# Early loads, copies of V, crossbar transposes and token-tile order in a sliding-window attention plus mixer kernel

## The chip, the cores and the metric

The kernel runs on one core of a Trainium2 chip. The metric is device time in microseconds (us); lower is better. Profiles are one execution each, and their span is some 1.7 us shorter than the device time of the same execution. "PE" is TensorE, "DVE" VectorE, "ACT" ScalarE, "POOL" GpSimd and "SP" SyncE. In this kernel POOL issues the loads (they change the type from float32 to bf16) and SP issues the stores and the crossbar transposes, which are transposes done by the DMA engines. A "landing" is the time from the issue of a DMA until its data has arrived; the "granted clock" is the TensorE clock that the throttle allowed, with 1.00 as full speed.

## The reference

For 8 batches of 576 tokens, 8 heads of 64 values, attention looks back over a window of 64 tokens. Its output x (8 x 576 x 512) goes through a low-rank mixing over tokens and then a two-layer channel mixer:

```python
scores = q @ k.T / 8;  mask: 0 <= pos_q - pos_k < 64;  attn = softmax(scores)
x = attn @ v                              # heads side by side: [8, 576, 512]
u = x + (x.T @ U @ V).T                   # U: [576, 32], V: [32, 576]
out = u + relu(u @ w_ch1) @ w_ch2         # 512 -> 2048 -> 512
```

## The kernel before

The mixer works on chunks of 512 tokens, 9 in all: 16 groups of 4 matmuls (`ch1`, result `psA`), then 16 groups of 4 (`ch2`, result `psU`). Between these groups, at "slots" 0 to 32, the program puts pieces of the attention of the next batch: scores `S`, masks `M`, `PV`, the low-rank product `U`, the addition `V`, and the transposes `UT` that make `uT`, the mixer's input. Attention of batch 0 runs alone at the start; chunk 0 carries batch 1, chunk 1 carries batch 2, and so on. Batches 0 and 1 have Q and K transposed on PE; from batch 2 on it is done by crossbar transposes (`TX`, `kf`/`qf`). From batch 3 on u is transposed by the crossbar too.

```python
    w1v = moe_w_ch1.rearrange("(c p) n -> p c n", p=P)
    for lo, hi in ((0, 1024), (1024, 2048)):
        nc.gpsimd.dma_start(out=w1b[:, :, lo:hi], in_=w1v[:, :, lo:hi])
    for t in range(NFULL):                       # V of batch 0, moved between partitions
        shift_v(0, nc.gpsimd.tensor_copy, range(t, t + 1))
    for _ in load_kq(1, False):
        pass
    load_v(1)
    w2v = moe_w_ch2.rearrange("(i p) m -> p i m", p=P)
    for i in range(0, NFC, 4):
        nc.gpsimd.dma_start(out=w2b[:, i : i + 4, :], in_=w2v[:, i : i + 4, :])
    for t in range(NFULL):
        shift_v(1, nc.gpsimd.tensor_copy, range(t, t + 1))
    # ... cut ...
        return [ch1(i) for i in range(NFC)] + [ch2(t, r) for t in range(TPC) for r in range(4)]
    # ... cut ...
    PLACE = {"S": [0, 0, 0, 3, 3], "M": [0, 1, 2, 4, 5], "PV": [8], "TX": [6, 7, 8, 9, 10],
             "U": [14], "V": [16, 17, 18], "UT": [17, 17, 18, 18, 19]}
    # PLACE_1 and PLACE_2 (chunks 0 and 1) cut: PV there in five pieces
    # ... cut ...
            if b == 1:
                for _ in load_kq(2, False):
                    pass
            if b + 1 < B:
                load_v(b + 1)
            if b + 2 < B:
                for _ in load_kq(b + 2, False):
                    pass
            # ... cut ...
            if NXB <= b + 1 < B:
                place(b + 1, ("T",), {"T": where["TX"]})    # Q/K transposes, one batch ahead
```

The softmax here doesn't subtract the row's maximum and nothing guards it: scores larger than these inputs give would overflow.

Of the kernel before, what the change touches and what calls it, by code (L numbers as in the profile page):

```python
# [16 lines left out]
def kernel(  # L17
# [26 lines left out]
    NXU = 3  # L44
# [15 lines left out]
    kg_pool = ctx.enter_context(tc.tile_pool(name="kg", bufs=4))  # L60
# [30 lines left out]
    kn = [const.tile([P, NT, H, D], BF16, name=f"kn{i}") for i in range(2)]  # L91
    qn = [const.tile([P, NT, H, D], BF16, name=f"qn{i}") for i in range(2)]

    kf = const.tile([P, NT * HP * P], BF16, name="kf")
    qf = const.tile([P, NT * HP * P], BF16, name="qf")
    kt, qt = ([f[:, j * S : (j + 1) * S] for j in range(HP)] for f in (kf, qf))
    kx, qx = (f.rearrange("p (t j w) -> p t j w", t=NT, j=HP) for f in (kf, qf))
    pts = const.tile([P, HP, 2, NB - 1, W], BF16, name="pts")
    ptl = const.tile([P, HP, 2, W], BF16, name="ptl")

# [3 lines left out]
    def load_kq(b, split):  # L104
        grouped = b < NGR
        if grouped:
            kb = kg_pool.tile([GP, H, GR, D], BF16, name="kg")
            qb = kg_pool.tile([GP, H, GR, D], BF16, name="qg")
        else:
            kb, qb = kn[b % 2], qn[b % 2]  # L110
        loaded[b] = (kb, qb)
        if grouped:
            step = 4 if split else H
            for h0 in range(0, H, step):
                hs = slice(h0, h0 + step)
                for t, src in ((kb, k), (qb, q)):
                    nc.gpsimd.dma_start(  # L117
                        out=t[:, hs, :, :].rearrange("p h c d -> p h (c d)"),
                        in_=src[b, hs, :, :].rearrange("h (p c) d -> p h (c d)", c=GR),
                    )  # L120
                    yield
# [24 lines left out]
    def shift_v(b, copy, tiles):  # L146
# [4 lines left out]
        if lo < last:  # L151
            copy(out=vb[0:W, lo:last, :, :], in_=va[0:W, lo + 1 : last + 1, :, :])  # L152

# [39 lines left out]
    for i in range(2):  # L193
        nc.vector.memset(kn[i][W:P, NFULL, :, :], 0.0)
        nc.vector.memset(qn[i][W:P, NFULL, :, :], 0.0)
# [22 lines left out]
    for t in range(NFULL):  # L218
        shift_v(0, nc.gpsimd.tensor_copy, range(t, t + 1))
    for _ in load_kq(1, False):  # L220
        pass
    load_v(1)
    w2v = moe_w_ch2.rearrange("(i p) m -> p i m", p=P)
    for i in range(0, NFC, 4):
        nc.gpsimd.dma_start(out=w2b[:, i : i + 4, :], in_=w2v[:, i : i + 4, :])
    for t in range(NFULL):
        shift_v(1, nc.gpsimd.tensor_copy, range(t, t + 1))
# [10 lines left out]
    def attention(b, spare=False):  # L238
# [6 lines left out]
        pcs = {}  # L245

# [29 lines left out]
        def TQ(j):  # L276
            def f():
                copy = nc.scalar.copy if spare and j == 3 else nc.vector.tensor_copy
                copy(out=place_of(qt, j), in_=tr(qb, j, b == 1))
# [81 lines left out]
        def SC8():  # L361
            if b >= NXU:
# [226 lines left out]
        def UT(t):  # L589
            def f():  # L590
                g = g0 + t
                dst = uT_of(g // TPC)[:, g % TPC, :, :]
                if b >= NXU:
# [16 lines left out]
        pcs["S"].insert(0 if b >= NXU else HP, SC8)  # L610
        if not spare:
            pcs["M"] = [MK(j) for j in range(HP)]
            pcs["M"].insert(0 if b >= NXU else HP, MK8)
        pcs["PV"] = [PVA] if b >= NXU else [PV(t) for t in range(NT)]
# [17 lines left out]
    DVE_RELU = {0: (8, 10, 11, 13, 15), 1: (2, 4, 6, 9, 10, 12, 13)}  # L632
    DVE_RELU_N = (0, 1, 2, 4, 5, 6, 8)

    def mlp(c):
# [3 lines left out]
        def ch1(i):  # L639
            def f():  # L640
                ps = psum["mm"].tile([P, CH], FP32, name="psA", tag="mm")
                for dc in range(NDC):
                    nc.tensor.matmul(  # L643
                        ps[:],
                        w1b[:, dc, i * P : (i + 1) * P],
                        uTc[:, :, dc, :],
                        start=(dc == 0),
                        stop=(dc == NDC - 1),
                    )
                c1[i] = c1_pool.tile([P, CH], BF16, name=f"c1_{i}")  # L650
                if i in DVE_RELU.get(c, DVE_RELU_N):
                    nc.vector.tensor_relu(out=c1[i][:], in_=ps[:])  # L652
                else:
                    nc.scalar.activation(out=c1[i][:], in_=ps[:], func=ACT.Relu)  # L654
# [25 lines left out]
        return [ch1(i) for i in range(NFC)] + [ch2(t, r) for t in range(TPC) for r in range(4)]  # L680
# [6 lines left out]
        "TX": [6, 7, 8, 9, 10],  # L687
# [6 lines left out]
        "T": [11, 11, 12, 12, 13, 13, 14, 14],  # L694
        "S": [12, 13, 14, 15, 15],
        "M": [13, 14, 15, 16, 16],
        "PV": [17, 17, 18, 19, 20],
        "U": [22],
        "V": [23, 24, 25],
        "UT": [25, 26, 27, 28, 29],  # L700
        "TX": [20, 22, 24, 26, 28],
    }
    PLACE_2 = {
        "S": [8, 8, 11, 11, 13],
        "M": [9, 10, 12, 13, 14],
        "PV": [16, 16, 18, 18, 20],
        "TX": [13, 14, 15, 16, 17],
        "U": [21],
        "V": [23, 24, 25],
        "UT": [25, 26, 27, 28, 29],  # L710
    }

# [3 lines left out]
    def turn_over(n, cols=CH):  # L716
# [17 lines left out]
    pair = maskA[:, 0, 1:3, :].rearrange("p (o n) w -> p o (n w)", o=1)  # L734
    nc.vector.tensor_copy(
        out=maskA[:, 0, 3:7, :].rearrange("p (o n) w -> p o (n w)", o=2),
        in_=pair.to_broadcast([P, 2, 2 * W]),
    )
    nc.vector.tensor_copy(out=maskA[:, 0, 7, :], in_=maskA[:, 0, 1, :])
    nc.vector.tensor_scalar(  # L740
        out=maskB[:],
        in0=maskA[:, 0, :, :],
# [4 lines left out]
    )  # L747
    order = "K0 K1 B0 B1 Q0 Q1 S0 S1 K2 K3 B2 Q2 B3 Q3 S2 S3 B4 S4"
    for what in order.split():
# [7 lines left out]
        turn_over({"B1": 1, "Q1": 1, "S1": 1, "Q3": 1}.get(what, 0))  # L757
# [88 lines left out]
```

## Time and profile before

The median of the first three runs is 321.33 us (321.08 to 322.29).

| stage of the profile | from, us | length, us | PE idle in it, us |
|---|---|---|---|
| start and batch 0 | 0 | 23.7 | about 6 |
| chunk 0 (with batch 1) | 23.69 | 40.82 | 2.64 |
| chunk 1 (with batch 2) | 64.51 | 33.80 | 0.27 |
| chunk 2 (with batch 3) | 98.31 | 33.35 | 1.20 |
| chunk 3 (with batch 4) | 131.66 | 32.10 | 0.10 |

The page of the kernel before begins with the span and the busy time of each engine; part 4 is the chain of waits that ended last.

```profile
span 319.2 us, 6811 instructions
PE 304.6 (95%) x2829; PEld 148.9 (47%) x2855; DVE 163.1 (51%) x293; ACT 101.8 (32%) x160; POOL 103.2 (32%) x134
...
PE 80%; DMA 13%; POOL 5%; issue 1%; DVE 0%; POOLq 0%
```

PE is the engine to watch, so what can be won is its idle time or its work. The stretches below are chunks 0 to 3 of the kernel before. The columns are the stretch, its length, the busy time of PE, PE's weight loads, DVE, ACT and POOL (each with its number of instructions), the granted clock, the DMA share and GB/s.

```profile
23.69:64.51 40.82, 38.18 (x418) 19.27 (x423) 22.50 (x38) 16.94 (x27) 24.75 (x32) 1.00 2.02 168
64.51:98.31 33.80, 33.53 (x316) 16.31 (x318) 20.46 (x35) 12.56 (x19) 18.45 (x22) 1.00 1.91 160
98.31:131.66 33.35, 32.15 (x301) 15.09 (x301) 19.31 (x33) 10.17 (x16) 16.02 (x20) 1.00 1.88 159
131.66:163.76 32.10, 32.00 (x299) 15.22 (x302) 18.37 (x31) 10.17 (x16) 17.12 (x21) 1.00 1.83 168
```

Length less PE busy is PE's idle time: 2.64 us in chunk 0 and 1.20 us in chunk 2, nearly none in chunk 3. The table of PE's waits of the kernel before says for what:

```profile
engine line waited for: us in total, times, longest us
PE psU L665 <- DMA w2b<-in_moe_w_ch_dram: 2.3, 3, 1.1
...
PE psA L643 <- DMA uTc<-un: 1.1, 1, 1.1
...
PE psA L643 <- ACT uTc L553: 0.5, 1, 0.5
```

The first is the second weight, w2, in chunk 0. In PE's timeline the three waits stand in square brackets, each before one quarter of w2:

```profile
44.57 1.02 PE L665 MATMUL psU<-w2b,c 128*128 128x512 bf16 x4 [0.33 <-DMA w2b<-in_moe_w_ch_dram]
...
47.09 1.02 PE L665 MATMUL psU<-w2b,c 128*128 128x512 bf16 x4 [0.86 <-DMA w2b<-in_moe_w_ch_dram]
...
49.63 1.02 PE L665 MATMUL psU<-w2b,c 128*128 128x512 bf16 x3 [1.13 <-DMA w2b<-in_moe_w_ch_dram]
```

The second is at 131.66 us, between chunks 2 and 3: the mixer waits for u's crossbar transposes. The third is at 23.69 us, before the first mixer matmul.

### The profile page before, as it was taken

The page shows a single profiled execution, that of the slowest core. Times are in us where ns is not written, and L with a number is a line of the kernel's source. Part 1 is how long each engine was busy: PE and PEld are TensorE (multiplying, and loading weights), DVE is VectorE, ACT ScalarE, POOL GpSimd, SP SyncE. Part 2 cuts the span into 40 slices and gives each one's busy share as a digit, 9 for nine tenths or more (in the row PEclk, how much of TensorE's full clock was granted, in tenths as well). Part 3 has the DMA queues.
Part 4 walks back from the last instruction along what each step waited for, and adds up shares of the span by engine and source line. Part 5 has one row for each costly group of instructions (what it writes and reads, how often), then busy time and mean ns, then how long its engine had stood idle before and what let it go on. Part 6 is the DMA issues. An engine that isn't in the chain of part 4 may idle for free.

```text
span 319.2 us, 6811 instructions
## 1 busy us (share of the span) xinstructions
PE 304.6 (95%) x2829; PEld 148.9 (47%) x2855; DVE 163.1 (51%) x293; ACT 101.8 (32%) x160; POOL 103.2 (32%) x134
## 2 busy tenths in 40 slices
PE   6879988999999999899999999999999999999995
PEld 6544543544454544354445444544454444444442
DVE  4464584537675854475647454756474443016011
ACT  2645550337124440345033502350245003201500
POOL 8591696645744744555543400000000000000000
PEclk9999999999999999999999999999999999999999
DMA  7999999999999999999999994444200520020011
GB/s 103 165 225 202 153 201 171 114 185 179 148 124 218 157 127 138 193 179 156 146 204 167 138 162 150 68 100 103 98 2 2 115 100 2 11 87 33 2 66 66
DMA packets 151871, 39.56 MB, mean 124 GB/s; under 512 B 140960, under 2 KB 146080, under 8 KB 151840
## 3 DMA queue, kind: packets, MB, share of 16 engines
q0 software_dynamic: 100096, 18.36, 82.2%
q1 hardware_dynamic: 51744, 20.77, 37.0%
q8 instruction: 22, 0.36, 0.5%
q14 instruction: 9, 0.07, 0.1%
HBM read 37.14 MB, written 9.44 MB: 146 GB/s over the span
## 4 chain that ended last, share of the span: by engine, by line
PE 80%; DMA 13%; POOL 5%; issue 1%; DVE 0%; POOLq 0%
PE psU L665 36%; PE psA L643 35%; DMA qg<-in_q_dram 5%; DMA vA<-in_v_dram 3%; DMA uTc<-un 3%; PE psv L566 2%; DMA qn<-in_q_dram 2%; PE sc L326 2%; PE xw L388 2%; POOL vB L149 1%; POOL vB L152 1%; PE xr L388 1%; PE pshh L487 1%; PE tpu L598 1%; POOL kg L117 1%
## 5 line engine op out<-in xcount | busy, mean ns | idle before, releaser
L665 PE MATMUL psU<-w2b,c 128*128 128x512 bf16 x555 | 130.3, 379 | 3.6 <-DMA w2b<-in_moe_w_ch_dram 2.3
L643 PE MATMUL psA<-uTc,w1b 128*128 128x512 bf16 x576 | 131.0, 380 | 1.6 <-DMA uTc<-un 1.1
L665 PEld LDWEIGHTS <-c 128*128 128x128 bf16 x576 | 55.2, 98 | 66.8 <-issue 3.0
L643 PEld LDWEIGHTS <-w1b 128*128 128x128 bf16 x576 | 54.0, 98 | 66.3 <-DMA uTc<-un 1.6
L654 ACT ACTIVATE c<-psA 128x512 bf16<-128x512 f32 x83 | 49.6, 597 | 91.3 <-PE psA L643 91.2
L674 DVE TENSOR_TENSOR osb<-psU,un 128x512 f32<-128x512 f32 x36 | 24.9, 691 | 82.9 <-PE psU L665 82.7
L652 DVE TENSOR_SCALAR c<-psA 128x512 bf16<-128x512 f32 x61 | 42.1, 690 | 25.8 <-PE psA L643 25.8
L579 DVE TENSOR_TENSOR un<-psv,xs 128x512 bf16<-128x512 f32 (+1 forms) x40 | 25.4, 683 | 22.1 <-PE psv L566 22.0
L135 POOL DMA_DIRECT2D vA<-in_v_dram x32 | 28.1, 888 | 19.8 <-DMA kn<-in_k_dram 6.4
L126 POOL DMA_DIRECT2D qn<-in_q_dram x30 | 25.3, 843 | 22.9 <-DMA vA<-in_v_dram 12.8
L346 ACT ACTIVATE pts<-sc 128x1024 bf16<-128x1024 f32 x32 | 31.4, 1028 | 2.3 <-PE sc L326 2.2
L126 POOL DMA_DIRECT2D kn<-in_k_dram x30 | 25.8, 859 | 15.9 <-DMA vA<-in_v_dram 9.4
L379 ACT ACTIVATE ptl<-low 128x256 bf16<-128x256 f32 x5 | 1.9, 384 | 65.8 <-PE high L326 65.8
L352 DVE TENSOR_TENSOR pts<-pts,maskA 128x1024 bf16<-128x1024 bf16 x28 | 19.1, 682 | 0.1
L326 PEld LDWEIGHTS <-kf 64*64 64x64 bf16 x704 | 9.9, 107 | 8.2 <-issue 8.0
L326 PE MATMUL sc<-qf,kf 64*64 64x128 bf16 (+1 forms) x624 | 12.1, 212 | 1.2 <-issue 0.4
L388 PEld LDWEIGHTS <-pts 128*64 128x64 bf16 x512 | 10.2, 110 | 6.1 <-issue 3.7
L566 PE MATMUL psv<-hh,vrep 128*128 128x512 bf16 x40 | 12.5, 379 | 0.0
L455 DVE TENSOR_TENSOR xs<-xw,rcw 128x896 bf16<-128x896 f32 x10 | 10.9, 1092 | 0.3
L411 DVE TENSOR_TENSOR xs<-xr,rcp 128x512 bf16<-128x512 f32 (+1 forms) x15 | 10.4, 690 | 0.5
L502 ACT CAST hh<-pshh 128x512 bf16<-128x512 f32 x7 | 4.1, 581 | 16.9 <-PE pshh L495 16.9
L601 ACT COPY uTc<-tpu 128x512 bf16<-128x512 bf16 x9 | 5.3, 586 | 11.2 <-PE tpu L598 11.2
(102 smaller groups left out, 159.7 us busy)
## 6 DMA issues: line engine op xcount, KB each, us to landing
out_dram<-osb SPq DMA_DIRECT2D x36, 256.0 KB, 2.4
vA<-in_v_dram POOLq DMA_DIRECT2D x32, 128.0 KB, 10.9
kn<-in_k_dram POOLq DMA_DIRECT2D x24, 128.0 KB, 12.5
qn<-in_q_dram POOLq DMA_DIRECT2D x24, 128.0 KB, 12.1
w1b<-in_moe_w_ch_dram POOLq DMA_DIRECT2D x2, 1024.0 KB, 16.3
w2b<-in_moe_w_ch_dram POOLq DMA_DIRECT2D x4, 512.0 KB, 12.8
kg<-in_k_dram POOLq DMA_DIRECT2D x2, 288.0 KB, 5.8
qg<-in_q_dram POOLq DMA_DIRECT2D x2, 288.0 KB, 6.6
```

Of the source, the lines that this page charges most:

```text
L126: nc.gpsimd.dma_start(out=dst[0:rows, t, :, :], in_=src[b, :, t * P : t * P + rows, :].rearrange("h p d -> p h d"),)
L135: nc.gpsimd.dma_start(out=va[:, t, :, 0:D], in_=v[b, :, t * P : (t + 1) * P, :].rearrange("h p d -> p h d"),)
L326: nc.tensor.matmul(sc[g][r0 : r0 + W, col * W : (col + n) * W], keys_of(j, u, rs), queries_of(j, blk, n, rs), start=not spare, stop=last o ...
L346: nc.scalar.activation(out=dst, in_=sc[:], func=ACT.Exp, scale=scale)
L352: nc.vector.tensor_tensor(out=dst, in0=dst, in1=maskA.rearrange("p g n w -> p g (n w)"), op=ALU.mult)
L388: nc.tensor.matmul(dst, pts[:, h // 2, h % 2, blk, :] if blk < NB - 1 else ptl[:, h // 2, h % 2, :], rhs, start=True, stop=True,)
L579: nc.vector.tensor_tensor(out=u_tiles[g][rs, :], in0=ps[0][rs, n, :], in1=x[rs, t, :, :].rearrange("p h d -> p (h d)"), op=ALU.add,)
L643: nc.tensor.matmul(ps[:], w1b[:, dc, i * P : (i + 1) * P], uTc[:, :, dc, :], start=(dc == 0), stop=(dc == NDC - 1),)
L652: nc.vector.tensor_relu(out=c1[i][:], in_=ps[:])
L654: nc.scalar.activation(out=c1[i][:], in_=ps[:], func=ACT.Relu)
L665: nc.tensor.matmul(acc[t][:], c1[i][:, t * P : (t + 1) * P], w2b[:, i, :], start=(i == 0), stop=(i == NFC - 1),)
L674: nc.vector.tensor_tensor(out=osb[:], in0=acc[t][:], in1=u_tiles[g][:], op=ALU.add)
```

## The change

Its intent is to take these early waits away and to give the transposes more room:

- w2 is loaded half before and half after V of batch 1; in chunk 0 `ch2` runs token tiles in pairs, so the later quarters of w2 are asked for later; the first two `ch1` tiles of chunk 0 are interleaved.
- Copies of V between partitions go from POOL, which issues the loads, to ACT and DVE.
- Loads of V2 and of K/Q of batch 3 are held until tile 2 and the last tile of batch 2's transposes have landed (a one-element copy on POOL that reads them).
- `kf`/`qf` get two buffers, and from batch 4 on Q/K are transposed two batches ahead.
- PV of batches 1 and 2 comes in one piece, as it did from batch 3 on.
- Batch 2's scores begin with the last 64 tokens, as they did from batch 3 on. In chunk 2 (batch 3) each piece of attention moves two slots later (`PLACE_3`).
- Mask copies of the start are moved off the way.

```diff
-    for t in range(NFULL):
-        shift_v(0, nc.gpsimd.tensor_copy, range(t, t + 1))
+    for t in range(2):
+        shift_high(0, nc.gpsimd.tensor_copy, t)
+        shift_low(0, nc.gpsimd.tensor_copy, t)
+    shift_low(0, nc.gpsimd.tensor_copy, 2)
     for _ in load_kq(1, False):
         pass
-    load_v(1)
     for i in range(0, NFC, 4):
+        if i == NFC // 2:
+            load_v(1)
         nc.gpsimd.dma_start(out=w2b[:, i : i + 4, :], in_=w2v[:, i : i + 4, :])
-    for t in range(NFULL):
-        shift_v(1, nc.gpsimd.tensor_copy, range(t, t + 1))
@@ mlp: ch1(*ids) runs its tiles interleaved @@
-        return [ch1(i) for i in range(NFC)] + [ch2(t, r) for t in range(TPC) for r in range(4)]
+        ups = [ch1(i) for i in range(NFC)]
+        if c == 0:
+            ups[0:2] = [ch1(0, 1), lambda: None]
+            return ups + [ch2(t, r) for u in (0, 2) for r in range(4) for t in (u, u + 1)]
+        return ups + [ch2(t, r) for t in range(TPC) for r in range(4)]
@@ places @@
+    PLACE_3 = {"S": [2, 2, 2, 5, 5], "M": [2, 3, 4, 6, 7], "SV": [7, 7, 8, 8], "PV": [10],
+               "U": [16], "V": [18, 19, 20], "UT": [19, 19, 20, 20, 21]}      # chunk 2
+    CROSS = {0: {2: [16, 17, 18, 19, 20]},                 # chunk: {batch: slots of its TX}
+             1: {3: [13, 14, 15, 16, 17], 4: [26, 27, 28, 29, 30]},
+             2: {5: [24, 25, 26, 27, 28]}}
+    CROSS_N = [20, 21, 22, 23, 24]
@@ loop @@
-            if NXB <= b + 1 < B:
-                place(b + 1, ("T",), {"T": where["TX"]})
+            for n, at in CROSS.get(c, {c + 3: CROSS_N}).items():
+                if n < B:
+                    place(n, ("T",), {"T": at})
+            if b == 1:                                     # after(t): POOL copies one element of qf tile t
+                slots[20] += [after(2), lambda: load_v(2), after(NT - 1), load_next]
```

(Cut: the buffers, the mask code, the order of the start, PLACE_1 and PLACE_2, the line that moves the last tokens' scores, and which engine does which ReLU. PLACE_3 and CROSS are written more tightly than in the file.)

More of the change, by code (lines that the diff above doesn't have):

```diff
@@ L43 @@
     NXB = 2
-    NXU = 3
+    NXT = 3
     GP = S // GR
@@ L59 @@
     const = ctx.enter_context(tc.tile_pool(name="const", bufs=1))
-    kg_pool = ctx.enter_context(tc.tile_pool(name="kg", bufs=4))
     uT_pool = ctx.enter_context(tc.tile_pool(name="uT", bufs=3))
@@ L90 @@
     vB = [const.tile([P, NFULL, H, VW], BF16, name=f"vB{i}") for i in range(2)]
-    kn = [const.tile([P, NT, H, D], BF16, name=f"kn{i}") for i in range(2)]
-    qn = [const.tile([P, NT, H, D], BF16, name=f"qn{i}") for i in range(2)]
-    kf = const.tile([P, NT * HP * P], BF16, name="kf")
-    qf = const.tile([P, NT * HP * P], BF16, name="qf")
-    kt, qt = ([f[:, j * S : (j + 1) * S] for j in range(HP)] for f in (kf, qf))
-    kx, qx = (f.rearrange("p (t j w) -> p t j w", t=NT, j=HP) for f in (kf, qf))
+    kr = [const.tile([P, H * GR * D], BF16, name=f"kr{i}") for i in range(2)]
+    qr = [const.tile([P, H * GR * D], BF16, name=f"qr{i}") for i in range(2)]
+    kn, qn = (
+        [r[:, 0 : NT * DM].rearrange("p (t h d) -> p t h d", t=NT, h=H) for r in rs] for rs in (kr, qr)
+    )
+    kfs = [const.tile([P, NT * HP * P], BF16, name=f"kf{i}") for i in range(2)]
+    qfs = [const.tile([P, NT * HP * P], BF16, name=f"qf{i}") for i in range(2)]
     pts = const.tile([P, HP, 2, NB - 1, W], BF16, name="pts")
     ptl = const.tile([P, HP, 2, W], BF16, name="ptl")
+    held = const.tile([1, 1], BF16, name="held")
     loaded = {}
@@ L106, in load_kq @@
         if grouped:
-            kb = kg_pool.tile([GP, H, GR, D], BF16, name="kg")
-            qb = kg_pool.tile([GP, H, GR, D], BF16, name="qg")
+            kb, qb = (
+                r[0:GP, :].rearrange("p (h c d) -> p h c d", h=H, c=GR) for r in (kr[b % 2], qr[b % 2])
+            )
         else:
@@ L112, in load_kq @@
         if grouped:
-            step = 4 if split else H
-            for h0 in range(0, H, step):
-                hs = slice(h0, h0 + step)
+            for h0, h1 in ((0, 4), (4, 8)) if split else ((0, H),):
+                hs = slice(h0, h1)
                 for t, src in ((kb, k), (qb, q)):
@@ L152, in shift_v, with shift_high, shift_low @@
             copy(out=vb[0:W, lo:last, :, :], in_=va[0:W, lo + 1 : last + 1, :, :])
+    def shift_high(b, copy, t):
+        copy(out=vB[b % 2][W:P, t, :, :], in_=vA[b % 2][W:P, t, :, :])
+    def shift_low(b, copy, t):
+        copy(out=vB[b % 2][0:W, t, :, :], in_=vA[b % 2][0:W, t + 1, :, :])
     kq0 = load_kq(0, True)
@@ L193 @@
     for i in range(2):
-        nc.vector.memset(kn[i][W:P, NFULL, :, :], 0.0)
-        nc.vector.memset(qn[i][W:P, NFULL, :, :], 0.0)
+        nc.vector.memset(kn[i][GP:P, NFULL, :, :], 0.0)
+        nc.vector.memset(qn[i][GP:P, NFULL, :, :], 0.0)
     nc.sync.dma_start(
@@ L245, in attention @@
         pcs = {}
+        kf, qf = kfs[odd], qfs[odd]
+        kt, qt = ([f[:, j * S : (j + 1) * S] for j in range(HP)] for f in (kf, qf))
+        kx, qx = (f.rearrange("p (t j w) -> p t j w", t=NT, j=HP) for f in (kf, qf))
         grouped = b < NGR
@@ L277, in f @@
             def f():
-                copy = nc.scalar.copy if spare and j == 3 else nc.vector.tensor_copy
-                copy(out=place_of(qt, j), in_=tr(qb, j, b == 1))
+                nc.vector.tensor_copy(out=place_of(qt, j), in_=tr(qb, j, b == 1))
             return f
@@ L361, in SC8 @@
         def SC8():
-            if b >= NXU:
+            if b >= NGR:
                 low = ps_tp.tile([P, CH], FP32, name="low", tag="tp")
@@ L592, in f @@
                 dst = uT_of(g // TPC)[:, g % TPC, :, :]
-                if b >= NXU:
+                if b >= NXT:
                     nc.sync.dma_start_transpose(out=dst, in_=u_tiles[g][:])
@@ L609, in attention @@
         pcs["B"] = [SB(j) for j in range(HP + 1)]
-        pcs["S"].insert(0 if b >= NXU else HP, SC8)
+        pcs["S"].insert(0 if b >= NGR else HP, SC8)
         if not spare:
             pcs["M"] = [MK(j) for j in range(HP)]
-            pcs["M"].insert(0 if b >= NXU else HP, MK8)
-        pcs["PV"] = [PVA] if b >= NXU else [PV(t) for t in range(NT)]
+            pcs["M"].insert(0 if b >= NGR else HP, MK8)
+        pcs["PV"] = [PVA] if not spare else [PV(t) for t in range(NT)]
         pcs["U"] = [UM((t,)) for t in range(NT)] if spare else [UM(tuple(range(NT)))]
@@ L629, in attention @@
         return pcs
-    DVE_RELU = {0: (8, 10, 11, 13, 15), 1: (2, 4, 6, 9, 10, 12, 13)}
+    DVE_RELU = {0: (7, 9, 11, 15), 1: (4, 7, 9, 10, 11, 13, 14), 2: (2, 3, 4, 6, 7, 8, 10)}
     DVE_RELU_N = (0, 1, 2, 4, 5, 6, 8)
@@ L637, in mlp, with ch1 @@
         c1 = [None] * NFC
-        def ch1(i):
+        def ch1(*ids):
             def f():
-                ps = psum["mm"].tile([P, CH], FP32, name="psA", tag="mm")
+                ps = {i: psum["mm"].tile([P, CH], FP32, name="psA", tag="mm") for i in ids}
                 for dc in range(NDC):
-                    nc.tensor.matmul(
-                        ps[:],
-                        w1b[:, dc, i * P : (i + 1) * P],
-                        uTc[:, :, dc, :],
-                        start=(dc == 0),
-                        stop=(dc == NDC - 1),
-                    )
-                c1[i] = c1_pool.tile([P, CH], BF16, name=f"c1_{i}")
-                if i in DVE_RELU.get(c, DVE_RELU_N):
-                    nc.vector.tensor_relu(out=c1[i][:], in_=ps[:])
-                else:
-                    nc.scalar.activation(out=c1[i][:], in_=ps[:], func=ACT.Relu)
+                    for i in ids:
+                        nc.tensor.matmul(
+                            ps[i][:],
+                            w1b[:, dc, i * P : (i + 1) * P],
+                            uTc[:, :, dc, :],
+                            start=(dc == 0),
+                            stop=(dc == NDC - 1),
+                        )
+                for i in ids:
+                    c1[i] = c1_pool.tile([P, CH], BF16, name=f"c1_{i}")
+                    if i in DVE_RELU.get(c, DVE_RELU_N):
+                        nc.vector.tensor_relu(out=c1[i][:], in_=ps[i][:])
+                    else:
+                        nc.scalar.activation(out=c1[i][:], in_=ps[i][:], func=ACT.Relu)
             return f
@@ L686 @@
         "PV": [8],
-        "TX": [6, 7, 8, 9, 10],
         "U": [14],
@@ L693 @@
     PLACE_1 = {
-        "T": [11, 11, 12, 12, 13, 13, 14, 14],
-        "S": [12, 13, 14, 15, 15],
-        "M": [13, 14, 15, 16, 16],
-        "PV": [17, 17, 18, 19, 20],
-        "U": [22],
-        "V": [23, 24, 25],
-        "UT": [25, 26, 27, 28, 29],
-        "TX": [20, 22, 24, 26, 28],
+        "T": [10, 10, 11, 11, 12, 12, 13, 13],
+        "S": [11, 12, 13, 14, 15],
+        "M": [12, 13, 14, 15, 16],
+        "SV": [16, 16, 17, 17],
+        "PV": [18],
+        "U": [23],
+        "V": [24, 25, 26],
+        "UT": [27, 28, 29, 30, 102],
     }
     PLACE_2 = {
-        "S": [8, 8, 11, 11, 13],
-        "M": [9, 10, 12, 13, 14],
-        "PV": [16, 16, 18, 18, 20],
-        "TX": [13, 14, 15, 16, 17],
-        "U": [21],
-        "V": [23, 24, 25],
-        "UT": [25, 26, 27, 28, 29],
-    }
+        "S": [9, 9, 9, 12, 12],
+        "M": [9, 10, 11, 13, 14],
+        "SV": [15, 15, 16, 16],
+        "PV": [18],
+        "U": [23],
+        "V": [24, 25, 26],
+        "UT": [27, 28, 29, 30],
+    }
+    PLACE_3 = {
+        "S": [2, 2, 2, 5, 5],
+        "M": [2, 3, 4, 6, 7],
+        "SV": [7, 7, 8, 8],
+        "PV": [10],
+        "U": [16],
+        "V": [18, 19, 20],
+        "UT": [19, 19, 20, 20, 21],
+    }
+    CROSS = {
+        0: {2: [16, 17, 18, 19, 20]},
+        1: {3: [13, 14, 15, 16, 17], 4: [26, 27, 28, 29, 30]},
+        2: {5: [24, 25, 26, 27, 28]},
+    }
+    CROSS_N = [20, 21, 22, 23, 24]
     unread = psum["spare"].tile([P, CH], FP32, name="unread", tag="spare")
@@ L733 @@
     )
-    pair = maskA[:, 0, 1:3, :].rearrange("p (o n) w -> p o (n w)", o=1)
-    nc.vector.tensor_copy(
-        out=maskA[:, 0, 3:7, :].rearrange("p (o n) w -> p o (n w)", o=2),
-        in_=pair.to_broadcast([P, 2, 2 * W]),
-    )
-    nc.vector.tensor_copy(out=maskA[:, 0, 7, :], in_=maskA[:, 0, 1, :])
     nc.vector.tensor_scalar(
-        out=maskB[:],
-        in0=maskA[:, 0, :, :],
+        out=maskB[:, 0:3, :],
+        in0=maskA[:, 0, 0:3, :],
         scalar1=30000.0,
@@ L747, with repeat @@
     )
+    def repeat(copy, mask):
+        pair = mask[:, 1:3, :].rearrange("p (o n) w -> p o (n w)", o=1)
+        copy(
+            out=mask[:, 3:7, :].rearrange("p (o n) w -> p o (n w)", o=2),
+            in_=pair.to_broadcast([P, 2, 2 * W]),
+        )
+        nc.vector.tensor_copy(out=mask[:, 7, :], in_=mask[:, 1, :])
+    repeat(nc.scalar.copy, maskB)
     order = "K0 K1 B0 B1 Q0 Q1 S0 S1 K2 K3 B2 Q2 B3 Q3 S2 S3 B4 S4"
@@ L756 @@
             load_low_rank()
-        turn_over({"B1": 1, "Q1": 1, "S1": 1, "Q3": 1}.get(what, 0))
-    nc.vector.tensor_copy(out=maskA[:, 1, :, :], in_=maskA[:, 0, :, :])
+        turn_over({"B1": 1, "Q1": 1, "S1": 1, "B2": 1, "Q3": 1}.get(what, 0))
     nc.scalar.copy(out=ub[0][:], in_=uf[0][:])
+    for t in range(2, NFULL):
+        shift_high(0, nc.scalar.copy, t)
     nc.scalar.copy(out=vrep[:, W : W + S], in_=vf[:])
@@ L770 @@
         f()
+    repeat(nc.vector.tensor_copy, maskA[:, 0])
+    nc.vector.tensor_copy(out=maskA[:, 1, :, :], in_=maskA[:, 0, :, :])
     first.close()
@@ L774 @@
     )
+    all_slots = [[[] for _ in range(NSLOT + 1)] for _ in range(NCH)]
     for c in range(NCH):
-        slots = [[] for _ in range(NSLOT + 1)]
+        slots = all_slots[c]
         def place(b, parts, where):
@@ L784, in place @@
                 for f, s in zip(att[b][part], where[part]):
-                    slots[s].append(f)
+                    all_slots[c + s // 100][s % 100].append(f)
         b = c + 1
@@ L791, with load_next @@
                     pass
-            if b + 1 < B:
-                load_v(b + 1)
-            if b + 2 < B:
+            def load_next(b=b):
                 for _ in load_kq(b + 2, False):
                     pass
-            where = {1: PLACE_1, 2: PLACE_2}.get(b, PLACE)
+            if 1 < b and b + 1 < B:
+                load_v(b + 1)
+            if 1 < b and b + 2 < B:
+                load_next()
+            where = {1: PLACE_1, 2: PLACE_2, 3: PLACE_3}.get(b, PLACE)
             if b < NXB:
@@ L802, with land, f, after @@
                 slots[6].append(lambda: nc.scalar.copy(out=ub[1][:], in_=uf[1][:]))
-            for bs, slot in ((b, 8), (b + 1, 24)):
-                if 1 < bs < B and (slot == 24) == (bs > 2):
-                    slots[slot].append(
-                        lambda bs=bs: shift_v(bs, nc.vector.tensor_copy, range(NFULL))
-                    )
-            place(b, ("S", "M", "PV"), where)
-            if NXB <= b + 1 < B:
-                place(b + 1, ("T",), {"T": where["TX"]})
-            place(b, ("U", "V", "UT"), where)
+            if 3 < b + 1 < B:
+                slots[24].append(
+                    lambda bs=b + 1: shift_v(bs, nc.vector.tensor_copy, range(NFULL))
+                )
+            if b <= 3:
+                def land(t, b=b):
+                    def f():
+                        shift_high(b, nc.scalar.copy, t)
+                        if t > 0:
+                            shift_low(b, nc.vector.tensor_copy, t - 1)
+                    return f
+                att[b]["SV"] = [land(t) for t in range(NFULL)]
+                place(b, ("SV",), where)
+            place(b, ("S", "M", "PV"), where)
+            for n, at in CROSS.get(c, {c + 3: CROSS_N}).items():
+                if n < B:
+                    place(n, ("T",), {"T": at})
+            place(b, ("U", "V", "UT"), where)
+            if b == 1:
+                def after(t):
+                    return lambda: nc.gpsimd.tensor_copy(
+                        out=held[:], in_=qfs[0][0:1, t * HP * P : t * HP * P + 1]
+                    )
+                slots[20] += [after(2), lambda: load_v(2), after(NT - 1), load_next]
         for fill, extra in zip(mlp(c) + [lambda: None], slots):
```

## The prediction

> **What bounds the kernel now.** TensorE. The page shows PE busy 304.6 of 319.2 us at full granted clock; 80% of the chain of waits is PE. Busy share alone proves little (the Trainium skill, "Trainium Kernel Development and Optimization", introduction: a bad metric, because matmuls are pipelined), so I go by the chain's start times: four 128x512 matmuls take 0.86 us, the mixer's 1152 then about 248 us (estimate). A steady chunk with attention takes 32.1 us (163.9 to 196.0), nearly without idle PE. Early chunks are worse: chunk 0 41 us (23.7 to 64.5), chunk 1 33.9, chunk 2 33.2.
>
> PE's idle time is 14.6 us (windows, table of waits): about 6 before 24 us (first loads, attention of batch 0); 2.3 in chunk 0, three waits for w2b between 44 and 50 us; 1.1 at 131 us, before chunk 3, for the crossbar transposes of u (landing 8.3 us there, median 4.0); 3.7 at the end; crumbs.
>
> **What the change does.**
> 1. Start: Q3's copy goes from ACT to DVE and mask copies leave the path, so the exponentials end about 0.35 us sooner; the interleaved first two channel tiles hide part of the 0.47 us wait for the last uT copies. Gain 0.6.
> 2. Chunk 0: w2's first half goes ahead of V1, and with token tiles in pairs its second half is needed later. The 2.3 us should go. PV of batch 1 in one piece costs 1.29 us (steady chunk) against about 1.9: gain 0.5; one u transpose moves to chunk 1 (0.22). Against it, ACT gets four 64x520 copies of V (about 0.5 us each, estimated from its other copies) just before PV: I count 12 to 13.8 us of ACT work against 12.3 of PE work there, so PV waits about 0.6. Net gain 2.4.
> 3. Chunk 1: PV in one piece (1.66 to 1.29), crumbs. Gain 0.4.
> 4. Chunk 2: batch 4's Q/K transposes no longer stand ahead of u's in the SP queue, nor share the DMA engines with as many loads ("DMA: Bandwidth & Descriptors", "Issuing engines are not separate DMA queues": all queues interleave on the same 16; the trace agrees: a Q/K transpose holds the SP queue 1.2 to 2.8 us, longest beside loads). Gain 1.1.
> 5. Chunks 3 to 8 and the tail: same PE work, nothing to remove: 0.
> Matmul counts are the same but for one filler.
>
> Sum 4.5 to 5.5 us, all on PE's path: **predicted 316.4 us, range 314.4 to 319.0**. Faster by over 2% (under 314.9): 0.14; within 2%: 0.84; slower: 0.02. Most of the reordering of loads buys only slack off the path.
>
> **What would show it.** Table of PE waits: w2b under 0.5 us; uTc gone. First mixer matmul near 23.1 instead of 23.7. Chunk 0 about 38.5 us, chunk 1 33.3, chunk 2 32.1, the others unchanged within 0.1. A new wait of PE in PV of batch 1, on ACT's copies into vB or on V1, up to 1 us. Batch 2's Q/K transposes end near 58 us instead of 69; batch 3's end near 80 instead of 93.
>
> **What would make it wrong.** Better: PV doesn't wait and chunk 0 has more slack than I see (41 us against about 37.5 of PE work); then 315. Worse: V1 lands after 42 us, which blocks ACT in order; the held loads make batch 3's transposes late for chunk 2, whose scores come at its slot 2; or batch 4's transposes block u's in the SP queue. Each would show as PE waiting for kf, qf or uTc, some us each.

## The result

The changed kernel took 317.89 us (median of 4 runs, 317.72 to 317.98), the kernel before 321.81 us (median of 4). The ratio is 0.9877, with a 95% interval of 0.9848 to 0.9905. Ratios here are the mean time of one kernel's fast runs over that of the other's of the same rounds, so not quite the ratio of the medians. The gain is clear of the noise but under the 2% from which a run is called faster here.

The page of the changed kernel:

```profile
span 316.0 us, 6876 instructions
PE 305.9 (97%) x2856; PEld 148.8 (47%) x2856; DVE 163.3 (52%) x297; ACT 109.5 (35%) x176; POOL 97.7 (31%) x127
...
PE 94%; DVE 2%; DMA 2%; issue 1%; ACT 0%; POOLq 0%
```

DMA has nearly gone from the chain. The same four chunks as above, in the changed kernel:

```profile
23.70:61.70 38.00, 37.58 (x419) 18.83 (x420) 23.36 (x42) 18.73 (x32) 12.15 (x15) 1.00 1.74 173
61.70:94.91 33.21, 33.21 (x323) 16.31 (x322) 18.80 (x33) 15.29 (x25) 23.82 (x30) 1.00 1.81 158
94.91:128.44 33.53, 32.45 (x302) 15.24 (x301) 19.98 (x36) 12.48 (x20) 16.05 (x20) 1.00 1.76 167
128.44:160.53 32.09, 32.09 (x301) 15.20 (x302) 18.29 (x31) 10.17 (x16) 15.39 (x19) 1.00 1.74 164
```

Chunk 0 got 2.82 us shorter and chunk 1 0.59 us. Chunk 2 did not get shorter (33.53 against 33.35), the start did not either (the first mixer matmul comes at 23.70 against 23.69), and from chunk 3 on nothing changed. The sum of 3.2 us is the whole difference of the two spans. The table of PE's waits of the changed kernel:

```profile
PE psA L655 <- DVE osb L687: 1.1, 1, 1.1
...
PE sc L337 <- issue: 0.9, 2, 0.4
...
PE psA L655 <- DVE uTc L564: 0.4, 1, 0.4
```

The waits for w2 are gone. The wait of 1.1 us before chunk 3 is still there, under another name: not u's transposes but DVE's `osb`, the addition that ends an output tile. Here are PE's timeline, then SP's timeline, then the landing times of the transposes into uT in this stretch, of the changed kernel:

```profile
128.44 1.02 PE L655 MATMUL psA<-uTc,w1b 128*128 128x512 bf16 x4 [1.08 <-DVE osb L687]
...
114.18 3.70 SPq L690 DMA_DIRECT2D out_dram<-osb  x2
117.94 7.78 SPq L605 DMA_TRANSPOSE uTc<-un  x5
...
DMA to landing us min/median/max: 7.1/7.7/7.8
```

Chunk 3 needs the first three of the five transposes. The third is issued near 120.6 us; 7.8 us later is 128.4 us, which is when chunk 3 starts. `osb` had ended 0.34 us before that. So there are two theories for this wait, u's third transpose or `osb`, and experiments 1, 8 and 12 decide between them.

### The profile page after: what moved, and what is told of

The parts are those of the page before. It is cut to its first block, busy times and chain, and to the rows that moved or that the text cites. A ratio compares the mean times of both kernels' runs of the same rounds, so it can differ in the third digit from the quotient of the medians.

```text
span 316.0 us, 6876 instructions
## 1 busy us (share of the span) xinstructions
PE 305.9 (97%) x2856; PEld 148.8 (47%) x2856; DVE 163.3 (52%) x297; ACT 109.5 (35%) x176; POOL 97.7 (31%) x127
## 4 chain that ended last, share of the span: by engine, by line
PE 94%; DVE 2%; DMA 2%; issue 1%; ACT 0%; POOLq 0%
PE psA L655 40%; PE psU L678 40%; PE sc L337 3%; PE psv L577 3%; PE xw L399 2%; DMA kr<-in_k_dram 2%; PE tpg L274 1%; PE pshh L498 1%; DVE qf L290 1%; PE sc L327 1%; PE tpu L609 1%; PE tpm L274 1%; PE xr L399 1%; DVE osb L687 0%; PE low L337 0%
## 5 line engine op out<-in xcount | busy, mean ns | idle before, releaser
L665 DVE TENSOR_SCALAR c<-psA 128x512 bf16<-128x512 f32 x60 | 41.3, 689 | 28.1 <-PE psA L655 28.1
L128 POOL DMA_DIRECT2D kr<-in_k_dram x30 | 25.3, 842 | 27.6 <-DMA vA<-in_v_dram 12.7
L128 POOL DMA_DIRECT2D qr<-in_q_dram x30 | 25.8, 859 | 16.4 <-DMA vA<-in_v_dram 8.7
L466 DVE TENSOR_TENSOR xs<-xw,rcw 128x896 bf16<-128x896 f32 x14 | 15.3, 1092 | 0.5
L399 PE MATMUL xw<-vA,pts 128*64 128x65 bf16 x217 | 8.5, 195 | 0.0
```

The costliest lines, as they stand in the source:

```text
L128: nc.gpsimd.dma_start(out=dst[0:rows, t, :, :], in_=src[b, :, t * P : t * P + rows, :].rearrange("h p d -> p h d"),)
L399: nc.tensor.matmul(dst, pts[:, h // 2, h % 2, blk, :] if blk < NB - 1 else ptl[:, h // 2, h % 2, :], rhs, start=True, stop=True,)
L665: nc.vector.tensor_relu(out=c1[i][:], in_=ps[i][:])
```

## The experiments

All are edits of the changed kernel; all gave right results. They ran on three chips: e1 and e3 to e5 on one, e12 on another, the rest on a third. The device times of one kernel spread by 0.8 to 4.3 us over its fast runs (one run of e11, at 323.45 us, was slow; the ratio leaves it out), as much as most effects here, so the verdicts rest on the lengths of the stages within each trace. A length is the difference of the start times of the first `psA` of two chunks in PE's timeline. Chunks from 3 to 6 lasted 32.1 us in every run.

| run | mixer starts | chunk 0 | chunk 1 | chunk 2 | of it wait for uT | median us (ratio to before) |
|---|---|---|---|---|---|---|
| before | 23.69 | 40.82 | 33.80 | 33.35 | 1.09 | 321.81 |
| changed | 23.70 | 38.00 | 33.21 | 33.53 | 1.08 | 317.89 (0.9877) |
| e0, changed again | 23.68 | 37.73 | 33.21 | 34.11 | 1.65 | 318.27 (0.9911) |
| e1 | 23.37 | 37.80 | 33.21 | 33.05 | 0.60 | 317.56 (0.9907) |
| e2 | 23.44 | 38.00 | 35.01 | 34.21 | 1.76 | 319.65 (0.9948) |
| e3 | 23.42 | 39.00 | 33.21 | 33.76 | 1.31 | 318.62 (0.9942) |
| e4 | 24.00 | 37.97 | 33.21 | 34.27 | 1.64 | 318.35 (0.9920) |
| e5 | 23.82 | 38.61 | 33.21 | 33.83 | 1.37 | 319.42 (0.9971) |
| e6 | 24.49 | 38.25 | 33.21 | 33.57 | 1.11 | 318.87 (0.9905) |
| e7 | 26.05 | 37.39 | 33.21 | 34.07 | 1.61 | 318.15 (0.9886) |
| e8 | 23.83 | 37.90 | 33.21 | 33.22 | 0.77 | 317.56 (0.9888) |
| e10 | 24.47 | 38.78 | 34.24 | 34.14 | 1.57 | 319.75 (0.9951) |
| e11 | 23.89 | 38.36 | 33.20 | 35.30 | 1.43 | 319.76 (0.9923) |
| e12 | 23.50 | 38.27 | 33.21 | 33.52 | none | 318.51 (0.9921) |

Two spreads need care. The start differs from run to run by up to 2.7 us in kernels whose start is the same. Of the three late ones, e6 and e7 had a lower granted clock (0.76 and 0.50 between 18 and 22 us); e10 had the full clock and a pause of 0.79 us in the scores of batch 0 (0.18 us in the control). And chunk 0 holds a pause in the scores at its slot 15 for which the trace names no releaser: none in e4, e5 and e7, 0.16 us in the control, 0.42 in the first profile, 0.44 in e3, 0.76 in e11. It is taken out below where it matters; its cause stays open.

### e0: control

No edit.

> The changed kernel once more, unedited, as the control for the runs beside it. Both theories: chunks 0, 1 and 2 last 38.0, 33.2 and 33.5 us as in its first profile, 32.1 from chunk 3 on, and one wait of 1.1 us before chunk 3; the time may lie some tenths off 317.9 on another chip.

Chunks 0 and 1 repeated; the wait before chunk 3 was 1.65 us this time. Over the nine profiles that leave chunk 2's end as it is (the changed kernel, e0, e2 to e5, e7, e10, e11) it lies between 1.08 and 1.76 us. An effect on it has to be seen against that.

### e3, e4 and e5: the order of loads and the pairs

```diff
 e3 and e5
-            return ups + [ch2(t, r) for u in (0, 2) for r in range(4) for t in (u, u + 1)]
+            return ups + [ch2(t, r) for t in range(TPC) for r in range(4)]
 e4 and e5
-        if i == NFC // 2:
+        if i == 0:
             load_v(1)
```

> The changed kernel with chunk 0's token tiles one after the other again; V1 stays between the halves of w2. Theory A (both parts are needed to take the 2.3 us of w2b waits away): the third and fourth quarter of w2 land at about 46.5 and 49.1 us and are asked for at about 45.8 and 48.4, so PE waits 0.7 to 1.5 us for w2b, time 318.6 to 319.4. Theory B (the order of the loads alone did it): no wait, time within 0.2 us of 317.9.

> The changed kernel with V1 loaded ahead of all of w2 again; token tiles stay in pairs. Theory A (both needed): the last two quarters land as late as in the kernel before or a little earlier (48 to 49.5 us) and pairs ask for them at 48.9 and 50.7, the first two quarters may be late instead for the first pairs: wait 0 to 1 us, time 317.9 to 318.9. Theory B (order of the loads alone did it): wait of about 2 us, time near 320.

> The changed kernel with both undone: V1 ahead of w2 and token tiles one after the other. If the two parts are what took the waits away, the 2.3 us of w2b waits come back, 1.8 to 2.6 us with what else was changed, and the time is 319.7 to 320.5, so these two parts carry more than half of the 3.9 us. If something else did it (no copies of V on POOL, earlier K/Q loads), the wait stays under 1 us.

PE's timeline around the end of w2, first in e3, where only the pairs are undone:

```profile
46.19 1.02 PE L678 MATMUL psU<-w2b,c 128*128 128x512 bf16 x4 [0.53 <-DMA w2b<-in_moe_w_ch_dram]
48.74 3.61 PE L678 MATMUL psU<-w2b,c 128*128 128x512 bf16 x16 [0.23 <-DMA w2b<-in_moe_w_ch_dram]
```

and in e5, where both are undone:

```profile
46.21 1.02 PE L678 MATMUL psU<-w2b,c 128*128 128x512 bf16 x4 [0.79 <-DMA w2b<-in_moe_w_ch_dram]
48.74 3.61 PE L678 MATMUL psU<-w2b,c 128*128 128x512 bf16 x16 [0.22 <-DMA w2b<-in_moe_w_ch_dram]
```

Without the pairs the waits are 0.76 us (e3) and 1.01 us (e5). With the pairs the waits for w2 are zero whether V1 comes first or not (e4). So the pairs are what takes the last 0.8 to 1.0 us, and putting half of w2 ahead of V1 is worth about 0.25 us of w2's waits without them and nothing with them. (e3's chunk 0 is still longer than e5's: of the 0.39 us, 0.44 us are the pause. And e4 has a wait of 0.38 us for Q of batch 1 that the others lack; e5, which loads V1 as early, does not have it, so its cause is not shown.) All this is one profile each. And even with both undone, 1.3 of the 2.3 us do not come back. Something else in the change had removed them, and my expectation for e5 missed this. The third quarter lands at 46.2 us in e5 against 47.1 in the kernel before, and the fourth at 48.7 against 49.6: 0.9 us earlier. POOL issued the K/Q loads of batch 1 at 17.95 us in the changed kernel against 18.90, because two copies of V had left its queue. Besides, PV in one piece stands between the third and the fourth quarter in e5 and gives the fourth time to land. The split between these two was not measured.

### e10: PV in pieces again

```diff
-        pcs["PV"] = [PVA] if not spare else [PV(t) for t in range(NT)]
+        pcs["PV"] = [PVA] if b > 2 else [PV(t) for t in range(NT)]
 PLACE_1, PLACE_2:  "PV": [18]  ->  "PV": [17, 18, 19, 20, 21]
```

> The changed kernel with PV of batches 1 and 2 in five pieces again (slots 17 to 21). If the one-piece form is worth what the traces show (1.30 us against about 1.9 and 1.66), chunk 0 grows by 0.4 to 0.7 us and chunk 1 by 0.3 to 0.5, time 0.7 to 1.2 us above the control. Rival: the pieces hide behind other work and cost nothing, time within 0.2 us; or they make PE wait for DVE's copies between them, which costs more than 1.2.

Chunk 0 grew by 1.05 us against the control, chunk 1 by 1.03, both more than expected, with no wait of PE in either but the pause (0.17 us). The chain in chunk 1 of e10 (start, length, what) shows why:

```profile
80.67 0.38 PE xr L399 x16
81.05 0.97 PE psU L678 x4
82.02 0.38 PE xr L399 x16
82.40 0.97 PE psU L678 x4
```

Four mixer matmuls take 0.86 us when they follow others of their kind and 0.97 us after a piece of PV. In the timelines it is not every other kind of work that costs this: the extra 0.11 us also follows the scores and the low-rank product, whose matmuls use part of PE's array (64\*64 and 128\*32 in the timeline, 128\*64 for PV), while after the pieces `V` (`psv`) and `UT` (`tpu`), which use 128\*128 like the mixer, it is 0.86 us again. Five pieces of PV cost that 0.11 us five times: 5 x 0.38 + 5 x 0.11 = 2.45 us, against 1.29 + 0.11 = 1.40 us in one piece, which is the 1.05 us. The kernel before had put some pieces into one slot, so the one-piece form gained less there: in chunk 1 1.66 + 3 x 0.11 - 1.40 = 0.59 us. The change of that chunk by 0.59 us includes an idle time of 0.27 us that went and a u transpose of 0.22 us that came.

### e2: without the hold

```diff
-                slots[20] += [after(2), lambda: load_v(2), after(NT - 1), load_next]
+                slots[20] += [lambda: load_v(2), load_next]
```

> The changed kernel without the hold: the loads of V2 and of K/Q of batch 3 are issued as soon as the buffers and the load queue allow, not after batch 2's transposes. Theory A (the hold buys slack only): batch 2's transposes end some us later than 64 us, but no new PE wait, time within 0.4 us of 317.9. Theory B (the hold is what keeps batch 2's and 3's transposes in time): PE waits for kf or qf in chunk 1 or 2, 1 us or more, time 319 or more.

My theory A fell. Chunk 1 grew by 1.8 us, and the wait is batch 2's transposes. PE's timeline of e2:

```profile
72.19 0.19 PE L337 MATMUL low<-qf,kf 64*64 64x64 bf16 x1 [1.73 <-DMA qf<-qr]
```

The DMA view gives the number of transposes issued between 49 and 66.5 us (batch 2's ten) and their median time to landing, first in the changed kernel:

```profile
kf<-kr SPq DMA_TRANSPOSE x5, 6.1
qf<-qr SPq DMA_TRANSPOSE x5, 5.3
```

and in e2:

```profile
kf<-kr SPq DMA_TRANSPOSE x5, 8.4
qf<-qr SPq DMA_TRANSPOSE x5, 8.0
```

SP is done with the last of them only 1.8 us later in e2 (65.94 against 64.12 us), but with the loads running beside them they take 2 to 3 us longer to land in the median. The kernel before had no hold, the same 8.4 us of landing, and no such wait. There are two reasons, and only one is the gain in chunk 0. Its chunk 1 began at 64.51 us, in e2 at 61.44. And it asked for the last tile of the transposes last, in its PE's timeline at

```profile
78.07 0.32 PE L326 MATMUL sc<-qf,kf 64*64 64x64 bf16 x16
```

while the changed kernel asks for it first, at 70.65 us. That is 7.4 us sooner: about 2.8 us by the earlier chunk and 4.6 us by the change's own order of batch 2's scores (13.56 against 8.95 us after the chunk's start). In e2 the last two transposes of Q were issued at 61.33 and 64.40 us and landed 8.0 and 7.7 us later, at 69.3 and 72.1; the scores wanted them at 70.46. So with the old order of scores the hold might not have been needed; that was not run. What e2 shows is that the change as it stands had used up the slack of the transposes, and that the hold gives it back.

### e11: the copies of V on POOL again

```diff
-    for t in range(2): ...                     # five copies on POOL
+    for t in range(NFULL):
+        shift_v(0, nc.gpsimd.tensor_copy, range(t, t + 1))
@@ after the loads of w2 @@
+    for t in range(NFULL):
+        shift_v(1, nc.gpsimd.tensor_copy, range(t, t + 1))
-            if b <= 3:
+            if 1 < b <= 3:                     # no copies of V1 on ACT and DVE
```

(ACT's two copies of V0 at the start are taken out too.)

> The changed kernel with the copies of V between partitions of batches 0 and 1 on POOL again, where POOL issues the loads. Theory A (POOL's copies delay the loads behind them): K/Q of batch 1 is issued 0.9 us later, K/Q of batch 2 some 4 us later, batch 2's transposes end near 68 us instead of 64 and land after its scores want them (71 us), so PE waits 1 to 2.5 us for qf or kf in chunk 1, and up to 0.9 us for w2b in chunk 0; time 1 to 3 us above the control. Theory B (the copies cost only slack): chunks 0 and 1 unchanged within 0.3 us.

K/Q of batch 2 was issued from 47.51 us instead of 40.16, and the cost came one stage later than I had expected. Batch 2's transposes just made it: with V2 and batch 3's loads still held, they landed in 4.6 and 5.1 us in the median. Then batch 3's loads started later (70.13 us against 67.48), SP issued batch 3's last transpose at 91.53 instead of 89.10 us, and the scores of batch 3 waited at the start of chunk 2. PE's timeline of e11:

```profile
99.56 0.19 PE L337 MATMUL low<-qf,kf 64*64 64x64 bf16 x1 [1.35 <-DMA qf<-qr]
```

So in this profile the copies cost 1.35 us in chunk 2, and in chunk 0, once the pause is taken out (0.76 us here, 0.16 in the control), nothing.

### e6: Q/K transposed one batch ahead again

```diff
-        1: {3: [13, 14, 15, 16, 17], 4: [26, 27, 28, 29, 30]},
-        2: {5: [24, 25, 26, 27, 28]},
+        1: {3: [13, 14, 15, 16, 17]},
+        2: {4: [6, 7, 8, 9, 10]},
-    CROSS_N = [20, 21, 22, 23, 24]
+    CROSS_N = [6, 7, 8, 9, 10]
-            for n, at in CROSS.get(c, {c + 3: CROSS_N}).items():
+            for n, at in CROSS.get(c, {c + 2: CROSS_N}).items():
```

> The changed kernel with Q/K transposes from batch 4 on issued one batch ahead, in slots 6 to 10 as in the kernel before, instead of two (the two sets of buffers stay). Theory A (two ahead buys only slack): chunk 2's wait for u's transposes stays between 0.8 and 1.6 us, chunks 3 to 8 are unchanged, time within 0.5 us of 317.9. Theory B (two ahead is what keeps later chunks free of waits): new waits for kf, qf or uTc in chunks 3 to 6, time over 319.

Chunks 1, 2 and 3 last 33.21, 33.57 and 32.09 us, as in the changed kernel; no new wait. Transposing two batches ahead, the part that needed new buffers, buys nothing that these runs show.

### e7: the first two tiles of chunk 0 not interleaved

```diff
-            ups[0:2] = [ch1(0, 1), lambda: None]
```

> The changed kernel with the first two channel tiles of chunk 0 one after the other again. Theory A (the first mixer matmul waits at 23.7 us for DVE's copy of the second uT quarter, because its weight load waits for DVE in both kernels, and after that nothing waits in either order): start at 23.7 us and time unchanged within 0.3 us. Theory B (the interleaving hides part of the copies, as predicted): time 0.2 to 0.5 us above 317.9.

The start of this profile was slowed by a lower clock, so its 26.05 us says nothing by itself, but the relation does. The first mixer matmul starts after DVE's copy of the second quarter of uT: the copy's end and the start are 23.52 and 23.69 us in the kernel before, 23.55 and 23.70 in the changed one, 24.34 and 24.49 in e6. Here they are in e7, from DVE's and PE's timelines:

```profile
25.22 0.69 DVE L564 CAST uTc<-uam 128x512 bf16<-128x512 f32 x1 [2.39 <-PE uam L555]
...
26.05 1.02 PE L655 MATMUL psA<-uTc,w1b 128*128 128x512 bf16 x4 [0.44 <-DVE uTc L564]
```

25.22 + 0.69 = 25.91, and 26.05 follows by 0.14 us. The order of the matmuls after that makes no difference: nothing waits after the first one. Chunk 0 is 37.39 us here, the shortest of all, so the interleaving has no measured gain. In the compiled programs, as I read them, the first weight load of the mixer waits for DVE and for the load of w1; no view here shows the first of these. Its accumulator takes over a bank from the start's tiles, which would explain the wait for DVE; that was not tested. The load of w1 is a second limit close by: in e4, e11 and e12 the page puts the wait on it (0.64 to 0.73 us), and there the first matmul starts 0.33 to 0.43 us after that copy, not 0.14 to 0.17.

### e1, e8 and e12: the wait before chunk 3

```diff
 e1    PLACE_3  -        "UT": [19, 19, 20, 20, 21],
                +        "UT": [18, 18, 19, 19, 20],
 e8    PLACE_3  -        "U": [16],  "V": [18, 19, 20],  "UT": [19, 19, 20, 20, 21],
                +        "U": [15],  "V": [17, 18, 19],  "UT": [17, 17, 18, 18, 19],
 e12   e8, and  -                if b >= NXT:
                +                if b >= NXT and not (b == 3 and t == 2):    # else: transpose on PE
```

> One edit to the changed kernel: batch 3's five crossbar transposes of u go one slot earlier, so the first two stand ahead of the store of output tile 0 in the SP queue. Theory A (the 1.1 us wait before chunk 3 is still for the third u transpose: issued near 120.6 us, landing 7.8 us, which is the 128.4 us at which the chunk starts; the store and the late slot hold it back): the wait falls to under 0.3 us, chunk 2 to about 32.3 us, time 0.8 to 1.1 us below the changed kernel's 317.9. Theory B (the page's label is right, the chunk waits for DVE's last osb, so for a PSUM bank): the wait stays at 1.1 us and the time at 317.9.

> The changed kernel with batch 3's whole end one slot earlier (low-rank matmul, addition to u, and u's crossbar transposes; the first four transposes ahead of the store of output tile 0). Moving two transposes alone halved the wait (0.6 us left) because the third still stood behind that store. Theory A (late issue of the third transpose): it is issued near 117.5 us, lands near 125.5, the wait is gone, chunk 2 lasts 32.4 us, time 0.9 to 1.2 us below the control. Theory B (the landing of 8 us beside the loads sets it, and earlier issue only makes the landing longer): a wait of 0.3 us or more stays.

> The changed kernel with batch 3's end one slot earlier as in e8, and one of u's five transposes, the third, done by TensorE (four 128x128 transposes, 0.22 us, as in chunks 0 and 1) instead of the crossbar. Theory A (the wait before chunk 3 is for that third transpose, which stands behind two others and lands 8 to 9 us after its issue beside the loads): the first two are issued by about 118.5 us and land before 127, so the wait is under 0.3 us, chunk 2 lasts 32.5 to 32.8 us against 33.5 to 34.1 of the changed kernel, time about 1 us below it, so it should beat both kernels. Theory B (the page's label: the chunk waits for DVE's last osb): the wait stays near 1 us and chunk 2 gets 0.2 us longer.

In e1 the wait fell to 0.60 us, in e8 to 0.77; both lie below all nine values of the unedited end, and neither is gone. SP's timeline of e1 shows the queue:

```profile
115.72 2.68 SPq L605 DMA_TRANSPOSE uTc<-un  x2
118.49 0.53 SPq L690 DMA_DIRECT2D out_dram<-osb  x1
119.11 5.71 SPq L605 DMA_TRANSPOSE uTc<-un  x3
```

The third transpose still stands behind a store that waits for its tile. In e8 it does not, but SP was busy with batch 4's last transpose and an older store until 116.16 us, 0.8 us after u's first tile was ready (115.38). Then four transposes held SP for 7.9 us (about 2 us each) and u's transposes landed 8.9 us after issue in the median, against 8.1 in the control. The third was issued at 119.3 us, not at 117.5 as I had expected (120.56 in the changed kernel); the issue got earlier and the landing longer. So theory B of that run is half right: beside the loads, earlier issue pays only in part.

In e12 the third transpose is done by PE and the wait at the chunk's start is gone altogether, while `osb` is still there. PE's timeline of e12, then DVE's:

```profile
116.83 0.40 PE L609 MATMUL tpu<-ident,un 128*128 128x128 bf16 x4 [0.82 <-DVE un L590]
...
128.50 1.03 PE L655 MATMUL psA<-uTc,w1b 128*128 128x512 bf16 x4
...
128.71 0.69 DVE L687 TENSOR_TENSOR osb<-psU,un 128x512 f32<-128x512 f32 x1 [2.76 <-PE psU L678]
```

Chunk 3 starts before its supposed releaser `osb` has even begun. That settles what the wait was: u's third transpose, in the changed kernel as in the kernel before. The label `osb` was only the last event that the page could see; the page of e1 names uTc for the same wait, that of e2 nothing. But e12 won nothing: I had placed PE's transposes directly behind the addition that makes u's tile, so PE waited 0.82 us for DVE there, and 0.82 + 0.22 us of new work eat the gain (33.52 us). Two slots later should do without that wait; it was not run.

No version clearly beats the changed kernel. e8 against the control on the same chip has medians of 317.56 and 318.27 us, six runs each, but the ranges (316.16 to 320.22 and 317.63 to 320.72) overlap. In the traces e1 and e8 save 0.3 to 1.1 us in chunk 2 against the two profiles of the changed kernel (33.53 and 34.11 us).

## Why the prediction was right, and where its steps failed

The time was right: 316.4 us was predicted with a range of 314.4 to 319.0, "within 2%" at 0.84, and 317.89 us was measured. Of its five terms three held (2, 3 and 5, though not 2's cause) and two failed (1 and 4). The range was wide enough to cover that: a gain of 4.5 to 5.5 us was predicted, the traces have 3.2 and the medians 3.9. That term 2 came out near its size is in part luck: PV gave more and ACT's copies cost less than I counted, and a pause of 0.42 us that nobody foresaw took some of it back.

1. **Start, predicted gain 0.6, measured 0.** The 0.35 us for the exponentials was not there: the last exponential of batch 0 started at 16.38 us against 16.35, because the scores before it came no earlier. The 0.2 to 0.3 us for the interleaving failed as e7 shows: the first matmul is the one that waits, and both orders have it.
2. **Chunk 0, predicted 2.4, measured 2.8.** The waits for w2 went, as predicted. But the cause I gave, order of loads and pairs, carries only 1.0 of 2.3 us (e5). PV in one piece was worth more than the 0.5 us I took, because I had left out the 0.11 us at each switch (e10). The 0.6 us of waiting that I charged to ACT's copies did not come: PV runs from 46.77 to 48.07 us, 1.30 us, without a pause.
3. **Chunk 1, predicted 0.4, measured 0.6.** Right. It holds only because of the hold (e2).
4. **Chunk 2, predicted 1.1, measured -0.2.** This is the step that failed. "Batch 4's Q/K transposes no longer stand ahead of u's in the SP queue" named a real delay, as SP's timeline of the kernel before shows:

```profile
118.48 1.66 SPq L285 DMA_TRANSPOSE qf<-qn  x1
120.23 7.13 SPq L594 DMA_TRANSPOSE uTc<-un  x4
```

u's first tile was ready at 117.7 us and waited 2.5 us for batch 4's. In the changed kernel these are done at 114.09 us. But I overlooked what the change does to u itself: it comes two slots later (the first tile is ready 21.3 us after the chunk's start, not 19.4) and stands behind a store (ready at 116.23, issued at 117.94). What counts is when the third u transpose is issued against when the chunk ends. It was issued 7.3 us before the end of chunk 2's matmuls in the kernel before (123.28 against 130.57 us) and 6.8 us in the changed kernel (120.56 against 127.36), and it lands nearly as slowly as before (7.8 us against 8.3); in both, that is longer than the time left.
5. **Chunks 3 to 8, predicted 0.** Right: 32.1 us in every run.

The sentence "most of the reordering of loads buys only slack off the path" was wrong for two of its three parts. The hold is worth 1.8 us in chunk 1 (with the change's order of batch 2's scores), and the copies taken off POOL 1.35 us in chunk 2. It holds for the two batches ahead (e6). I had judged slack by the kernel before, where chunk 1 starts 2.8 us later and asks for the last tile 4.6 us later in the chunk. The dates I gave for the transposes were too early for the same reason of a queue I had not followed: batch 2's end at 64 us, not 58, and batch 3's at 91, not 80, since POOL issues K/Q of batch 2 from 40.2 to 51.5 us, with pauses for earlier loads to land.

The rule behind the hold is in the Trainium skill, "DMA: Bandwidth & Descriptors", section "Issuing engines are not separate DMA queues": DMAs of different issuing engines run on the same 16 engines and interleave. The traces agree, with a median landing of `qf` of 5.3 us while loads are held and 8.0 beside them. I had cited it for chunk 2 and not applied it to chunk 1.

## What to carry to other kernels

When a change takes a wait out of one stage, the next stage starts earlier by that much, and what was just in time for it can be late, the more so if the change also asks for it in another order: give the slack back there (here by holding loads that nobody needs yet), or the gain moves on as a new wait. Ask for a late-arriving operand later, by another order of the work, before you try to load it sooner. And check the name of a wait against the issue and landing times of the DMAs around it: a wait that changes its label and not its length is probably the same wait.

## What the Trainium skill lacked or had wrong

- "DMA: Bandwidth & Descriptors", section "Issuing engines are not separate DMA queues", says that issue time on the sequencer is usually small relative to the DMA itself. For crossbar transposes of one 128 x 512 tile it is not beside loads: u's hold SP's queue for 1.2 to 3.3 us each against 7 to 9 us of landing, and five of them in a row hold the queue for 7.8 us.
- No page that I read gives the landing time of a 128 x 512 crossbar transpose beside loads of small pieces. Here the medians are 5.3 and 6.1 us with the loads held and 8.0 and 8.4 us with them (changed kernel against e2).
- "TensorE: Matmul & The Clock Gate", section "Wait — 56ns, not 53.3ns?", gives the start-to-start time of matmuls of one kind; the traces agree for 512 columns (four in 0.86 us). It lacks the cost in time of a switch: the first four mixer matmuls after matmuls on part of the array (PV, scores, low-rank product) take 0.97 us, 0.11 us more each time (e10), and after others on 128 x 128 they do not.
- No page that I read explains the pauses of PE that end without a releaser in the trace, 0.2 to 0.8 us in the scores of chunk 0 in most runs and absent in others.
